# Where the lower half of V's token sums stands: partition 1, written by a transfer, or partition 32, written in place

## The chip, the cores and the metric

The kernel runs on one core of a Trainium2 chip. The time is device microseconds for one execution; lower is better. A core has TensorE (PE in the profile; its weight loads are the row PEld), VectorE (DVE), ScalarE (ACT), GpSimd (POOL) and the queue SP, from which this kernel issues all its transfers. The profile is one execution recorded on the chip.

## The reference, cut to what matters

Two stages follow each other. The first is attention with a bucket mask, for 4 batches and 8 heads of 768 tokens with 64 columns each; the second is a mixture of 4 causal attention experts on the result, per batch, of which each token uses two.

```python
q_bits = (np.einsum('bhsd,dk->bhsk', q, proj) > 0)          # six sign bits: a bucket of 64
mask = q_bucket[:, :, :, None] == k_bucket[:, :, None, :]
scores = scale * np.matmul(q, k.transpose(0, 1, 3, 2))
scores = np.where(mask, scores, -1000000000.0)
scores = scores - np.max(scores, axis=-1, keepdims=True)
attn = np.exp(scores)
attn = attn / (np.sum(attn, axis=-1, keepdims=True) + 1e-09)
return np.matmul(attn, v)
...
logits = x @ w_gate                                          # second stage, per expert e:
scores = np.where(causal, -1000000000.0, scale * (q @ k.transpose(0, 2, 1)))
ye = a @ v @ wo[e]                                           # a: softmax of scores
out += mask[..., None] * w[:, :, kk:kk + 1] * ye
```

One detail matters here. A query whose bucket holds no key has the same score for every key, so its result is the plain mean of V over the 768 tokens. The kernel marks such queries with a flag, and at the end of each head adds flag times (sum of V over the tokens) to the numerator and flag times 768 to the denominator.

## The kernel before, in words

**Units.** The work is cut into 48 units: 32 heads of the first stage (kind "L") and 16 experts of the second (kind "M"). They run in the order of `seq` (line 1393): first the heads of batch 0 by themselves, then the heads of a batch mixed with the experts of the batch before. Two neighbouring heads make a pair, which shares its loads, its scales and its V.

**One unit on TensorE.** The 768 queries and keys are six tiles of 128. `max_steps` (line 959) makes the scores of a unit two units ahead in PSUM tiles `mx`, of which there are two, and VectorE reduces each to row maxima (`pm`, or `pmw` for the first eight heads, which work in fp32). `shift_steps` turns the maxima into rows (`negm`, `row` or `roww`) and, for heads, into flags. `s_unit` (line 1075) makes the scores again with the keys on the partitions, in PSUM tiles `st`, of which there are three; ScalarE takes the exponential twice (`p` in fp32, `ph` in fp16) and GpSimd forms the remainder `pl` = p - ph. Some chunks after that (`LAG` = 4) the products with V follow, into the PSUM tile `o`: `ph` and `pl` with V's upper half `vh`, `ph` with its lower half `vl`. With the last chunk of a head, six more matmuls `o<-vs,fq` add the flagged queries' share (line 1155), and `normalise` divides and frees `o`.

**V's token sums.** `prep_v` (line 907) prepares V once for each pair, 16 times in all. It splits V into halves, sums each over the tokens by matmuls with a column of 2^-10 (`ones`), copies the 128 sums to `vcol`, transposes this column to a row, and writes the row's upper half to partition 0 of `vs` (type fp16). The remainder goes to a row `vsl` on partition 0, and a transfer of 256 bytes carries it to partition 1 of `vs`. The lines are 937 to 944. Two sets of `vs` take turns.

**Flags.** `flags` (line 1014) compares the transposed maxima of 12 rows (two copies of six tiles) and a transfer writes them to partitions 0 and 1 of `fq`, 768 queries wide. All other partitions of `fq` and `vs` are zero from the beginning, so `o<-vs,fq` runs over all 128 partitions and adds upper and lower half in one go.

**The order.** The program does not issue as it is written. A `Recorder` collects every operation with what it reads and writes, and `schedule` (line 310) plays it through on paper: each engine's time for each operation (`_cost`), delays between engines (`LAT`, `WAIT`), the number of buffers, and a priority. On each engine the operations are then issued in the planned order, and every engine works through its own list without overtaking. A transfer also moves one shared clock of the planner on, `dma`, by its size (line 254 and line 395):

```python
run = big.shape[-1] * (2 if big.dtype == HF else 4)
o.dma = prod(big.shape) * (2 if big.dtype == HF else 4) / 360.0 * (2 if run < 512 else 1)
...
dma = end = max(dma, st + 1275.0) + o.dma
```

The planner sees operands as `View`s, and a slice of partitions keeps its first and last one but not its step (line 57):

```python
p0, p1, _ = k[0].indices(self.shape[0])
return self._then("__getitem__", (key,), {}, (self.part[0] + p0, self.part[0] + p1), self.idx[k[1:]])
```

Almost every instruction has line 427 in the profile, since they are all issued there; so tiles, and not lines, tell them apart.

Of the kernel before, what the change touches and what calls it, by code (L numbers as in the profile page):

```python
# [10 lines left out]
FT = mybir.dt.float32  # L11
FR = mybir.dt.float32r
BF = mybir.dt.bfloat16
HF = mybir.dt.float16
I32 = mybir.dt.int32
AF = mybir.ActivationFunctionType
OP = mybir.AluOpType
# [443 lines left out]
def tile_kernel(ctx, tc, q, k, v, proj, w_gate, wq, wk, wv, wo, out):  # L461
    nc = Recorder(tc.nc, loose=("misc",))
    B, HP, _, _, HS = q.shape
    E, Dm, D = wq.shape
    H, S = 2 * HP, 2 * HS
    NB = proj.shape[1]
    NT = S // 128
# [5 lines left out]
    con = Pool(nc, ctx.enter_context(tc.tile_pool(name="con", bufs=1)), 1, 0)  # L473
    sb = Pool(nc, ctx.enter_context(tc.tile_pool(name="sb", bufs=2)), 2, 0)
# [3 lines left out]
    def misc():  # L478
        return psum.tile([128, 512], FT, name="misc", bufs=2)
# [32 lines left out]
    ident = con.tile([128, 128], FT, name="ident")  # L512
# [71 lines left out]
    RW = con.tile([128, 4], FT, name="rw")  # L584
    VS = [con.tile([128, 2, 66], HF, name=f"vs{i}") for i in range(NV)]
    FQ = [con.tile([128, S], HF, name=f"fq{i}") for i in range(3)]
    NM = [con.tile([128, 12, NT], FT, name=f"negm{i}") for i in range(3)]
    tri = con.tile([128, E, E], FT, name="tri")
    rows01 = con.tile([3, 128], HF, name="rows01")
# [12 lines left out]

    def constants():

        for t in NM + FQ:
            nc.gpsimd.memset(t, 0.0)
        for t in PM:
            nc.gpsimd.memset(t, -CLIP)
        nc.gpsimd.memset(NMW, 0.0)
        nc.gpsimd.memset(lower, 1.0 / UNIT)  # L610
        nc.gpsimd.memset(lower[0:NT], 0.0)
        nc.gpsimd.memset(rows01, UNIT)
        nc.gpsimd.memset(rows01[0:1], 0.0)
        for t in VS:
            nc.gpsimd.memset(t, 0.0)
            nc.gpsimd.memset(t[0:1, 0, 0:2], S / 1024.0)
            nc.gpsimd.memset(t[0:1, 1, 64:66], S / 1024.0)
        for t in VH + VF:
            nc.gpsimd.memset(t[:, :, 0:2], 1.0)
            nc.gpsimd.memset(t[:, :, 130:132], 1.0)  # L620
        for t in MVHS:
            nc.gpsimd.memset(t[:, :, :, 64:66], 1.0)
        nc.gpsimd.memset(mask_n, 0.0)
        nc.gpsimd.affine_select(out=mask_n, in_=mask_n, compare_op=OP.is_ge, fill=-BIG, base=0,
                                pattern=[[-1, 128]], channel_multiplier=1)
        nc.gpsimd.memset(mask_t, 0.0)
        nc.gpsimd.affine_select(out=mask_t, in_=mask_t, compare_op=OP.is_ge, fill=-BIG, base=0,
                                pattern=[[1, 128]], channel_multiplier=-1)
        nc.gpsimd.memset(ones, 2.0 ** -10)
        nc.gpsimd.memset(tri, 0.0)  # L630
        for e in range(1, E):
            nc.gpsimd.memset(tri[:, e, 0:e], 1.0)
# [272 lines left out]
    npair = [0]  # L905

    def prep_v(b, hp):
        nat = NAT.pop(("v", b, hp))
        c = CS[b % 2][:, hp, 2:3]
        if not b and hp < 2:  # L910
            mx = sb.tile([128, 1], BF, name="mx")
            nc.gate = marks["row"]
            nc.vector.tensor_reduce(mx, nat.rearrange("p h s -> p (h s)"), axis=AX.X, op=OP.max,
                                    apply_absolute_value=True)
            nc.gate = None
            yield 0
            scale_of([mx], c, 10)
            yield 213
        vs, vh, vl, vf = (t[npair[0] % NV] for t in (VS, VH, VL, VF))
        npair[0] += 1  # L920
        for h in range(2):
            cv = vf[:, :, 2 + D * h:2 + D * h + D]
            nc.scalar.activation(cv, nat[:, h].rearrange("p (j d) -> p j d", j=NT), AF.Copy, scale=c)
            hv = vh[:, :, 2 + D * h:2 + D * h + D]
            nc.scalar.activation(hv, cv, AF.Copy)
            nc.gpsimd.tensor_tensor(vl[:, :, h], cv, hv, op=OP.subtract)
            if not h:
                yield 0
        for h in range(2):
            U["L", b, 2 * hp + h].update(vf=vf[:, :, 66 * h:66 * h + 66], vh=vh[:, :, 66 * h:66 * h + 66], vl=vl[:, :, h], first=2 - 2 * h, den=64 * h,  # L930
                                         order=[2 * (i % 3) + i // 3 for i in range(NT)], c=c, vs=vs[:, h])
        yield 0
        p = misc()
        for n in range(2 * NT):
            x = vl[:, n // 2].rearrange("p h d -> p (h d)") if n % 2 else vh[:, n // 2, 2:2 + 2 * D]
            nc.tensor.matmul(p[:, 0:1], x, ones[:, 0:1], start=not n, stop=n == 2 * NT - 1)
        col = sb.tile([128, 1], FT, name="vcol")
        nc.copy(col, p[:, 0:1])
        nc.tensor.transpose(p[0:1, 128:256], col, ident)
        tv, to = p[0:1, 128:128 + 2 * D], vs.rearrange("p h c -> p (h c)")[:, 2:2 + 2 * D]  # L940
        nc.copy(to[0:1], tv)
        vsl = sb.tile([1, 2 * D], HF, name="vsl", bufs=1)
        nc.vector.tensor_tensor(vsl, tv, to[0:1], op=OP.subtract)
        nc.sync.dma_start(to[1:2], vsl)
        yield 450


# [66 lines left out]
    def flags(d, p):  # L1014
        fr = sb.tile([2 * NT, 128], HF, name="fr")

        if "wide" in d:
            nc.vector.tensor_scalar(fr, p[0:2 * NT, 0:128], WIDE / 2, 1024.0, op0=OP.is_ge, op1=OP.mult)
        else:
            nc.choose(("scalar", "activation", (fr, p[0:2 * NT, 0:128], AF.Relu), dict(scale=2.0 ** -18, bias=-1024.0)),  # L1020
                      ("vector", "tensor_scalar", (fr, p[0:2 * NT, 0:128], CLIP, 1024.0), dict(op0=OP.is_ge, op1=OP.mult)))
        d["fq"] = FQ[nflag[0] % 3]
        nflag[0] += 1
        nc.sync.dma_start(d["fq"][0:2].rearrange("p (j s) -> p j s", j=NT), fr[:, None, :])

    def shift_steps(u):
        d = U[u]
        lsh = u[0] == "L"
        nm = NM[nshift[0] % 3]
        nshift[0] += 1  # L1030
# [38 lines left out]
        if lsh:  # L1069
            flags(d, p)  # L1070
# [343 lines left out]
    for b in range(B):  # L1414
        for hp in range(HP):
            i = pos["L", b, 2 * hp]
# [17 lines left out]
            i = max(pos["L", b, 2 * hp + 1] + 1, i6 + 1 + XTS * hp)  # L1434
# [3 lines left out]
        for e in range(E):  # L1438
            i = pos["M", b, e]
# [5 lines left out]
        i = pos["M", b, E - 1]  # L1445
# [136 lines left out]
```

## Time and profile before

| | |
|---|---|
| median of 3 runs | 619.33 us (618.9 to 621.45) |
| the profiled execution's own time | 619.93 us |
| its span, first to last instruction | 618.2 us |
| TensorE busy | 603.7 us, 98% of the span |
| VectorE, ScalarE, GpSimd busy | 499.4, 501.0, 478.4 us (81%, 81%, 77%) |
| mean clock granted to TensorE | 0.994 of full |
| share of the 16 DMA engines taken by transfers | 30.2% |

The span is shorter than the execution by 1.7 us, which lie outside the first and last instruction. A busy row counts the time in which at least one instruction of the engine was under way; matmuls overlap each other, so one of 193 ns does not occupy TensorE for 193 ns. "idle before, releaser" tells how long an engine stood still ahead of an instruction and what ended that; "granted clock" (PEclk) is the share of full speed at which TensorE was allowed to run.

### The profile page before, as it was taken

How to read it: one execution, taken by the hardware profiler on the slowest of the kernel's cores; microseconds unless marked ns; L12 is line 12 of the kernel's file. 1: busy time of each engine (PE TensorE's matmuls, PEld its weight loads, DVE VectorE, ACT ScalarE, POOL GpSimd, SP SyncE). 2: the span in 40 equal slices, each digit the busy share in tenths (PEclk: the TensorE clock that was granted, in tenths of full speed). 3: DMA queues.
4: the chain of work that ended last, by engine and by line, in shares of the span. 5: the costliest groups of instructions: out<-in, count | busy, mean ns of one | idle time of the engine just before them, and what ended most of it. 6: DMA issues, size and time to landing. Idle time of an engine off the chain costs nothing.

```text
span 618.2 us, 20738 instructions
## 1 busy us (share of the span) xinstructions
PE 603.7 (98%) x7938; PEld 446.0 (72%) x7938; DVE 499.4 (81%) x1217; ACT 501.0 (81%) x1107; POOL 478.4 (77%) x535
## 2 busy tenths in 40 slices
PE   8989999999999999999999999999999999999996
PEld 5678787877777676777676777777776767767673
DVE  5866999999879998988888998996987877446753
ACT  2678799999959898977978989986988978933783
POOL 8788899998948898976976889884995868940560
PEclk9989999999999999999999999999999999999999
DMA  6765722233310414222242413222232221011212
GB/s 188 199 178 135 160 61 96 66 104 97 101 45 23 127 38 128 62 74 49 73 126 68 132 47 106 54 88 65 66 92 83 61 54 29 3 27 47 67 70 103
DMA packets 42931, 52.45 MB, mean 85 GB/s; under 512 B 15081, under 2 KB 32593, under 8 KB 42833
## 3 DMA queue, kind: packets, MB, share of 16 engines
q1 hardware_dynamic: 42833, 51.14, 30.2%
q8 instruction: 62, 1.02, 0.7%
q14 instruction: 36, 0.29, 0.1%
HBM read 20.98 MB, written 6.29 MB: 44 GB/s over the span
## 4 chain that ended last, share of the span: by engine, by line
PE 86%; ACT 5%; DVE 4%; DMA 2%; issue 1%; POOL 1%; SPq 0%; POOLq 0%; ACTq 0%; DVEq 0%
PE misc L427 25%; PE st L427 24%; PE o L427 23%; PE mx L427 14%; ACT p L427 2%; ACT ph L427 2%; DVE pm L427 1%; DMA vs<-vsl 1%; DVE qk L427 1%; POOL pl L427 1%; DMA qk<-Mw 1%; DMA qk<-M 1%; ACT xt L427 0%; DVE yn L427 0%; DVE xt L427 0%
## 5 line engine op out<-in xcount | busy, mean ns | idle before, releaser
L427 POOL TENSOR_TENSOR pl<-p,ph 128x512 f16<-128x512 f32 x368 | 415.7, 1154 | 105.3 <-ACT ph L427 59.3
L427 ACT ACTIVATE p<-st 128x512 f32<-128x512 f32 x372 | 223.9, 602 | 29.9 <-PE st L427 22.6
L427 ACT ACTIVATE ph<-st 128x512 f16<-128x512 f32 x372 | 223.6, 604 | 0.1
L427 DVE TENSOR_REDUCE pm<-mx 128x2 f32<-128x512 f32 (+2 forms) x344 | 203.7, 609 | 19.9 <-PE mx L427 18.9
L427 PE MATMUL st<-qk 128*128 128x256 f16 (+13 forms) x928 | 215.3, 325 | 0.9 <-ACT ph L427 0.6
L427 PEld LDWEIGHTS <-ph 128*128 128x128 f16 x2880 | 151.4, 98 | 26.0 <-issue 4.2
L427 PEld LDWEIGHTS <-qk 78*128 78x128 f16 (+4 forms) x1248 | 111.3, 98 | 49.4 <-issue 4.2
L427 PEld LDWEIGHTS <-pl 128*128 128x128 f16 x1440 | 131.5, 97 | 7.2 <-POOL pl L427 2.7
L427 PE MATMUL mx<-qk 76*128 76x512 f16 (+2 forms) x464 | 129.9, 328 | 1.3 <-DMA qk<-Mw 0.9
L427 PE MATMUL o<-vh,ph 128*128 128x65 f16 (+1 forms) x1104 | 120.1, 194 | 0.5 <-DVE yn L427 0.4
L427 PE MATMUL o<-vh,pl 128*128 128x65 f16 (+1 forms) x1104 | 119.2, 194 | 1.1 <-POOL pl L427 1.0
L427 PE MATMUL o<-vl,ph 128*128 128x64 f16 x1104 | 118.9, 192 | 0.0
L427 PE MATMUL misc<-xt,wqk_h 128*128 128x384 f16 x256 | 54.1, 325 | 0.0
L427 DVE TENSOR_REDUCE pmw<-mx 128x2 f32<-128x512 f32 x68 | 45.3, 681 | 5.8 <-PE mx L427 5.3
L427 PEld LDWEIGHTS <-xt 128*128 128x128 f16 x324 | 30.7, 97 | 10.1 <-DVE pm L427 0.6
L427 PE MATMUL o<-mvh,ph 128*128 128x65 f16 x336 | 36.8, 194 | 0.6 <-DVE yn L427 0.6
L427 PE MATMUL o<-mvh,pl 128*128 128x65 f16 x336 | 36.8, 193 | 0.0
L427 PE MATMUL o<-mvl,ph 128*128 128x64 f16 x336 | 36.7, 192 | 0.0
L427 PEld LDWEIGHTS <-ident 128*128 128x128 bf16 x339 | 28.1, 101 | 10.7 <-issue 2.4
L427 PEld LDWEIGHTS <-wqk_h 128*128 128x128 f16 x256 | 24.3, 97 | 14.6 <-DVE mvl L427 0.2
L427 ACT ACTIVATE qk<-misc 128x384 f16<-128x384 f32 x27 | 13.4, 497 | 23.7 <-PE misc L427 20.2
L427 POOL TENSOR_TENSOR vl<-vf,vh 128x384 f16<-128x384 f32 x32 | 30.4, 954 | 2.6 <-ACT vh L427 2.6
(205 smaller groups left out, 976.9 us busy)
## 6 DMA issues: line engine op xcount, KB each, us to landing
qk<-qk SPq DMA_DIRECT2D x128, 96.0 KB
natv<-in_v_dram SPq DMA_DIRECT2D x16, 384.0 KB
natq<-in_q_dram SPq DMA_DIRECT2D x15, 384.0 KB
natk<-in_k_dram SPq DMA_DIRECT2D x15, 384.0 KB
out_dram<-ot SPq DMA_DIRECT2D x20, 256.0 KB
qk<-qk SPq DMA_DIRECT2D x96, 48.0 KB
xt<-xt SPq DMA_DIRECT2D x16, 96.0 KB
xt<-xt SPq DMA_DIRECT2D x8, 192.0 KB
```

Source lines behind the costliest of these rows:

```text
L427: getattr(getattr(self.nc, e), m)(*[real(x) for x in args], **{k: real(x) for k, x in kw.items()})
```

## The change

The row that the transposition leaves in PSUM becomes 33 partitions high instead of one, with the sums on partitions 0 and 32 and zeros between. For that the column becomes a tile of 33 columns (two constant tiles `vcol0` and `vcol1`, set to zero at the start, which take turns), and the copy writes the sums to its columns 0 and 32. After the transposition one copy writes the 33 rows to `vs`, and VectorE subtracts on partition 32, in place: what stands there in fp16 is replaced by the remainder. The transfer and the row `vsl` are gone. The flags' transfer now writes partitions 0 and 32 of `fq`.

```diff
     FQ = [con.tile([128, S], HF, name=f"fq{i}") for i in range(3)]
+    VC = [con.tile([128, 33], FT, name=f"vcol{i}") for i in range(2)]
...
-        for t in NM + FQ:
+        for t in NM + FQ + VC:
             nc.gpsimd.memset(t, 0.0)
...
-        col = sb.tile([128, 1], FT, name="vcol")
-        nc.copy(col, p[:, 0:1])
-        nc.tensor.transpose(p[0:1, 128:256], col, ident)
-        tv, to = p[0:1, 128:128 + 2 * D], vs.rearrange("p h c -> p (h c)")[:, 2:2 + 2 * D]
-        nc.copy(to[0:1], tv)
-        vsl = sb.tile([1, 2 * D], HF, name="vsl", bufs=1)
-        nc.vector.tensor_tensor(vsl, tv, to[0:1], op=OP.subtract)
-        nc.sync.dma_start(to[1:2], vsl)
+        col = VC[npair[0] % 2]
+        nc.copy(col[:, 0:33:32], p[:, 0:1].to_broadcast([128, 2]))
+        nc.tensor.transpose(p[0:33, 128:256], col, ident)
+        tv, to = p[0:33, 128:128 + 2 * D], vs.rearrange("p h c -> p (h c)")[0:33, 2:2 + 2 * D]
+        nc.copy(to, tv)
+        nc.vector.tensor_tensor(to[32:33], tv[32:33], to[32:33], op=OP.subtract)
         yield 450
...
-        nc.sync.dma_start(d["fq"][0:2].rearrange("p (j s) -> p j s", j=NT), fr[:, None, :])
+        nc.sync.dma_start(d["fq"][0:33:32].rearrange("p (j s) -> p j s", j=NT), fr[:, None, :])
```

## The prediction, as it was put down before the changed kernel ran

> **What bounds the kernel now.** I read the share of busy time first, then what TensorE waited for, then the chain of waits around the one wait that has to do with this change, and last the busy time by stretches there.
>
> ```profile
> span 618.2 us, 20738 instructions
> PE 603.7 (98%) x7938; PEld 446.0 (72%) x7938; DVE 499.4 (81%) x1217; ACT 501.0 (81%) x1107; POOL 478.4 (77%) x535
> ```
>
> TensorE is the bound: it stands still for 618.2 - 603.7 = 14.5 us in all. The waits of TensorE, longest first (us in total, times, longest):
>
> ```profile
> PE o L427 <- DMA vs<-vsl: 2.0, 1, 2.0
> PE o L427 <- DVE ident L427: 1.8, 1, 1.8
> PE st L427 <- ACT ph L427: 1.1, 4, 0.4
> PE o L427 <- POOL pl L427: 1.0, 2, 0.6
> PE o L427 <- DVE yn L427: 1.0, 3, 0.6
> PE mx L427 <- DMA qk<-Mw: 0.9, 1, 0.9
> ...
> PE mx L427 <- DMA qk<-M: 0.2, 1, 0.2
> ```
>
> The longest wait of the run is for the very transfer that the change removes, and it occurs once, though there are 16 such transfers. The timeline shows where:
>
> ```profile
> 35.11 0.27 DVE L427 TENSOR_TENSOR vsl<-misc,vs 1x128 f16<-1x128 f32 x1
> 36.03 0.57 SPq L427 DMA_DIRECT2D vs<-vsl  x1
> 39.11 0.48 PE L427 MATMUL mx<-qk 76*128 76x512 f32 x1
> 41.62 0.34 PE L427 MATMUL o<-vs,fq 128*128 128x66 f16 x6 [2.03 <-DMA vs<-vsl]
> ```
>
> This is the end of the first head. The remainder of V's sums was ready at 35.11 + 0.27 = 35.38 us; the transfer was issued at 36.03, and TensorE's next instruction, the flagged queries' share, could start only at 41.62. In the chain of waits the transfer has one piece, from 36.03 for 5.54 us:
>
> ```profile
> 36.03 5.54 DMA vs<-vsl
> ```
>
> Later pairs have their sums long before a head ends, so nobody waits there. Now the stretches around it (length; busy time and instructions of PE, PEld, DVE, ACT, POOL; granted clock; DMA share; GB/s):
>
> ```profile
> core 0: us, PE busy (x) PEld busy (x) DVE busy (x) ACT busy (x) POOL busy (x), PEclk, DMA share, GB/s
> 24.95:28.37 3.42, 2.54 (x18) 1.93 (x17) 2.42 (x5) 3.42 (x10) 2.52 (x4) 1.00 0.47 127
> 36.00:39.59 3.59, 3.59 (x49) 2.92 (x46) 2.75 (x8) 3.59 (x8) 3.59 (x4) 1.00 0.92 297
> 39.59:41.62 2.03, 0.00 (x1) 0.00 (x1) 0.72 (x2) 2.03 (x5) 2.03 (x4) 1.00 0.53 130
> 41.62:42.02 0.40, 0.40 (x8) 0.40 (x8) 0.02 (x1) 0.06 (x1) 0.40 (x2) 1.00 0.74 181
> 42.02:48.84 6.82, 6.82 (x62) 5.49 (x61) 4.16 (x11) 2.46 (x7) 2.78 (x3) 0.50 0.56 141
> 48.84:52.25 3.41, 3.41 (x39) 3.00 (x36) 2.31 (x4) 3.29 (x8) 3.17 (x3) 1.00 0.53 117
> ```
>
> The stall has a second price. Just after it, from 42.02 to 48.84 us, TensorE's clock is 0.50, and it comes back without any other event. In those 6.82 us ScalarE is busy for 2.46 and GpSimd for 2.78, so TensorE sets the pace, at half speed: 6.82 x 0.5 = 3.41 us of its work is lost. The stretch begins 0.40 us after the stall ended. Mean clock over the span is 0.994 (the table above), a loss of some 0.006 x 618.2 = 3.7 us: there is no second such stretch of that size.
>
> **The change part by part.** *Removed: the transfer, and the wait for it.* The last producer of `vs` becomes VectorE's subtraction, ready at about 35.4 us; TensorE is there at 41.62 - 2.03 = 39.59, with 4.2 us to spare. The stall of 2.03 us goes. Without it nothing in that place holds TensorE still, so I take the half clock to go with it: 3.41 us. Together 5.44 us, the upper end of the gain.
>
> The lower end is what the other engines allow. They have to do the same work in a stretch of 9.25 us (39.59 to 48.84) that would shrink to 9.25 - 5.44 = 3.81. Their idle time in it: VectorE 9.25 - (0.72 + 0.02 + 4.16) = 4.35, ScalarE 9.25 - (2.03 + 0.06 + 2.46) = 4.70, GpSimd 9.25 - (2.03 + 0.40 + 2.78) = 4.04. The rows with the gaps:
>
> ```profile
> 39.62 0.69 DVE L427 TENSOR_REDUCE pmw<-mx 128x2 f32<-128x512 f32 x1
> 42.00 0.22 DVE L427 TENSOR_SCALAR rden<-o,cs 128x6 f32<-128x6 f32 x1 [1.68 <-PE o L427]
> 46.59 0.28 DVE L427 CAST vs<-misc 1x128 f16<-1x128 f32 x1 [1.97 <-PE misc L427]
> 45.38 0.93 POOL L427 TENSOR_TENSOR vl<-vf,vh 128x384 f16<-128x384 f32 x1 [1.51 <-ACT vh L427]
> 49.08 2.28 POOL L427 TENSOR_TENSOR pl<-p,ph 128x512 f16<-128x512 f32 x2 [2.77 <-ACT ph L427]
> ```
>
> So what is late next is VectorE: after the stall it normalises the head (`rden`, `xp`) ahead of the next row maxima, and it can begin this at 39.62 + 0.69 = 40.31 instead of 42.00, only 1.69 us earlier. TensorE has two `mx` tiles, so it feels VectorE soon; GpSimd's remainders are used some chunks later (`LAG`), so its 4.04 us bind less. The gain lies between 4.04 and 5.44 us; I take 4.9, the middle of VectorE's 4.35 and 5.44.
>
> *Removed: 16 issues on SP.* The two kinds of transfers as the tiles' instructions list them (ns least, median, most of the issue):
>
> ```profile
> L427 SPq DMA_DIRECT2D vs<-vsl x16: 552/555/893, 36.0 to 504.1; - x16
> L427 SPq DMA_DIRECT2D fq<-fr x32: 643/698/723, 21.1 to 517.0; - x32
> ```
>
> What stands behind each on SP is issued up to 0.57 us earlier. TensorE's only other wait for a transfer after that point is `qk<-M`, 0.2 us: the gain is 0 to 0.2, taken as 0. The flags' transfer keeps its pieces (12 rows of 256 bytes) and only its target partitions move. The trace shows no transfer to partitions 0 and 32, so I bound its issue by 0.55 us (`vs<-vsl`) and twice its own 0.70, and its landing by the 5.54 us above. No row of TensorE's waits names it, and the first one is issued at 21.1, 18 us ahead of its use: nothing, either way; if that cover were gone, it would cost what `vsl` costs now.
>
> *Changed in size.* Groups by shape (busy us, mean ns, idle before), and one row of a tile's instructions (ns least, median, most):
>
> ```profile
> L427 ACT ACTIVATE vcol<-misc 128x1 f32<-128x1 f32 x11 | 2.4, 220 | 3.9 <-PE misc L427 3.9
> L427 PEld LDWEIGHTS misc<-ident,vcol 128*1 128x1 f32 x16 | 1.4, 85 | 1.3 <-ACT vcol L427 1.0
> L427 PEld LDWEIGHTS misc<-ident,negm x48: 112/114/118, 20.0 to 589.8; 128*72 128x72 f32 x48
> L427 ACT ACTIVATE vs<-misc 1x128 f16<-1x128 f32 x10 | 2.6, 262 | 1.2 <-PE misc L427 1.2
> L427 ACT ACTIVATE fr<-misc 12x128 f16<-12x128 f32 x22 | 5.6, 252 | 0.0
> ```
>
> A column load of 33 lies between those of 1 (85 ns) and 72 (114): at most 0.03 us, 16 times 0.5 us. The copy of 33 rows of 128 instead of one costs the same, as 12 rows take 252 ns against 262 for one; the copy of two columns for one the same 220. The subtraction keeps its shape (0.27 us) and its engine; its result now releases TensorE with no transfer between. The trace shows no subtraction of this shape on partition 32: between 0 and one more instruction's length, 0.27 us, under cover of the 4.2 us to spare in the first pair and of whole heads in the others. I take 0.
>
> [...]
>
> *Added: two memsets on GpSimd at the start.* Bounds: 0.11 us (the 72 columns of `negm`, 0.33 for three) below, 0.2 for both above.
>
> ```profile
> 8.19 0.33 POOL L427 MEMSET negm<- 128x72 f32 x3
> 14.57 1.00 POOL L427 TENSOR_TENSOR qk<-natq,qk 128x384 fp32r<-128x384 f32 x1 [1.18 <-ACT qk L427]
> ```
>
> The first work behind them that others need starts after a wait of 1.18 us for ScalarE: hidden. Without that cover it costs at most 0.2 us.
>
> *The order.* The planner counts 33 partitions for the flags' slice, since it drops the step. With 768 columns of 2 bytes, divided by 360 and doubled for runs of 256 bytes, its price goes from 2 x 768 x 2 / 360 x 2 = 17 ns to 33 x 768 x 2 / 360 x 2 = 282 ns, 32 times, and 16 issues of 570 ns vanish from its SP. So all engines' orders from 21 us on may come out a little different, on paper only. That costs nothing by itself; what a new order can do on the chip is the open term: at best a part of the other waits above (1.1 + 1.0 + 1.0 + 0.9 + 0.2 = 4.2 us, of which I allow a third, 1.3), at worst new stalls like the one at 39.59, 5.44 us each.
>
> The sum against the profiled execution: 619.93 - 4.9 = 615.0. The median is 0.60 below that execution, so 619.33 - 4.9 = 614.4.
>
> **The rivals.**
>
> *The half clock stays, chance 0.09.* The stall goes, but the clock falls for another reason. For it: in 24.95 to 28.37 TensorE stood still for 3.42 - 2.54 = 0.88 us and the clock held, so not every gap does it, and I have a single case. Against it: the fall comes 0.40 us after the longest gap inside the kernel. Time: 619.33 - 2.03 = 617.3. [...]
>
> *One new stall, chance 0.17.* The new order brings another instruction of TensorE too early for its data. For it: the new planner prices above, and thin places such as `qk<-M`, already waited for by 0.2 us. Against it: in 48 units only six rows of TensorE's waits reach 0.9 us in total. Time: 619.33 - 4.9 + 2.03 = 616.5 if the clock holds, 619.33 - 4.9 + 5.44 = 619.9 if not.
>
> *Slower: the new order breaks the cover of the pair's first transfers, chance 0.18.* Place: the signs `qk<-M` that go ahead of a new pair's row maxima. If these slip by 2 us behind other transfers on SP, TensorE stands still as it did at 39.59 and pays the half clock as well, 5.44 us each. One such place gives 619.9, no change; it decides from two, with 619.33 - 4.9 + 10.88 = 625.3. For it: the 0.2 us already there. Against it: there are 16 issues fewer ahead of them on SP.
>
> *The change does not do what it says, chance 0.06.* TensorE stands still at the same instruction, for the flags or a subtraction that the planner put off behind row maxima. Against it: 18 us and 4.2 us to spare. Time: unchanged, 619.3.
>
> **How the numbers follow.** The forecast, 614.4, has 0.50; the four rivals the other 0.50. Its own range is 613.3 to 616.5: below, 619.33 - 5.44 - 0.2 with 0.4 for the runs' lower spread (618.9); above, 619.33 - 4.04 with 1.2 for half of the upper spread. The whole range goes to 612.0 (the 1.3 us of a luckier order) and to 620.5 (one new stall with its half clock, 619.9, and 0.6 of spread); outside lies mainly the slower rival. A measurement of this kernel can tell about 0.5%, 3.1 us, from no change: faster means below 616.2, slower above 622.4. Faster: nearly all of the forecast (0.48) and a few hundredths of the one stall with full clock: 0.52. Slower: 0.18. Within 0.5%: the rest, 0.30.
>
> **What would show each step.** TensorE's waits have no row with `vs`; `o<-vs,fq` of the first head starts right behind a matmul of `mx`, near 39.6 us; the stretches from there to 49 us have clock 1.00 (the 3.41 us are right) or 0.50 (first rival). If the gain is below 4.0 us with full clock, VectorE or GpSimd shows no idle time from 40 to 45. The copy of 33 rows takes 0.25 to 0.28 us, the column's load 0.09 to 0.11. The prediction is wrong if TensorE has a new wait of 1 us or more behind 42 us, or a half-clock stretch elsewhere.

## The result, and the profile after

The changed kernel takes 626.22 us (median of 15 executions, 623.04 to 631.36) against 621.45 us of the kernel before, run beside it (15, 618.54 to 631.82). The ratio is 1.0106, 95% interval [1.0076, 1.0136]: slower by about 1%, where 4.9 us less were forecast. Its profiled execution took 624.08 us. The ratio is not that of these two medians, because executions at a lower clock that take over 1.5% more than their kernel's fastest are left out of it (and out of the medians in the table below, and the profiles of experiments e1 and e7, which are of that kind, are not read).

The share of busy time after the change:

```profile
span 622.3 us, 20709 instructions
PE 602.4 (97%) x7938; PEld 443.4 (71%) x7938; DVE 504.3 (81%) x1212; ACT 503.8 (81%) x1112; POOL 477.0 (77%) x537
```

TensorE stands still for 622.3 - 602.4 = 19.9 us, 5.4 more than before. What it waited for (us in total, times, longest):

```profile
PE mx L427 <- DVE pm L427: 3.6, 8, 0.9
PE mx L427 <- DMA xt<-Mw: 1.9, 1, 1.9
...
PE misc L427 <- DVE negm L427: 1.4, 1, 1.4
...
PE mx L427 <- DMA qk<-M: 0.4, 1, 0.4
```

The row with `vs` is gone. The largest new rows are three: the row maxima wait for VectorE eight times (3.6 us), once for the sign bits of a wide pair (one of those that work in fp32; 1.9), and once `negm` is late (1.4). The stretches tell where. First of the kernel before, then of the one after (length; busy time and instructions of PE, PEld, DVE, ACT, POOL; granted clock; DMA share; GB/s):

```profile
30.00:48.00 18.00, 15.97 (x207) 13.08 (x199) 12.21 (x32) 11.02 (x25) 13.30 (x13) 0.83 0.65 172
48.00:62.00 14.00, 13.94 (x178) 11.68 (x177) 9.05 (x18) 13.75 (x29) 12.72 (x12) 0.97 0.52 132
...
107.00:150.00 43.00, 42.83 (x576) 32.58 (x575) 41.24 (x95) 41.57 (x97) 40.02 (x39) 1.00 0.35 93
```

```profile
30.00:48.00 18.00, 17.88 (x269) 15.42 (x265) 14.35 (x33) 16.86 (x38) 17.04 (x17) 1.00 0.75 198
48.00:62.00 14.00, 10.88 (x123) 7.52 (x123) 8.99 (x17) 9.30 (x19) 11.86 (x12) 1.00 0.71 189
...
107.00:150.00 43.00, 39.76 (x539) 29.28 (x536) 41.90 (x86) 41.10 (x95) 39.27 (x38) 1.00 0.28 74
```

Length less TensorE's busy time is its standstill. From 30 to 48 us it falls from 2.03 to 0.12, and the clock is full: the part that was forecast. From 48 to 62 it rises from 0.06 to 3.12, and from 107 to 150 from 0.17 to 3.24. The sum over the span: standstill +5.4 us; no half clock in the middle of the kernel, -3.4; and TensorE busy for 602.4 us at full clock against 603.7 - 3.41 = 600.3 before, +2.1. Together +4.1, which is 622.3 - 618.2. The 2.1 us are read from matmuls whose ends are modelled; the first after a wait shows its whole length (0.38 us for `mx`) where in a stream the next one starts 0.22 us later, so a part of them belongs to the new waits, and the rest stays open.

### The profile page after: what moved, and what is told of

The parts are those of the page before. It is cut to its first block, busy times and chain, and to the rows that moved or that the text cites. A ratio compares the mean times of both kernels' runs of the same rounds, so it can differ in the third digit from the quotient of the medians.

```text
span 622.3 us, 20709 instructions
## 1 busy us (share of the span) xinstructions
PE 602.4 (97%) x7938; PEld 443.4 (71%) x7938; DVE 504.3 (81%) x1212; ACT 503.8 (81%) x1112; POOL 477.0 (77%) x537
## 3 DMA queue, kind: packets, MB, share of 16 engines
q8 instruction: 62, 1.02, 0.7%
## 4 chain that ended last, share of the span: by engine, by line
PE 72%; DVE 15%; ACT 6%; issue 2%; DMA 2%; POOL 1%; SPq 0%; DVEq 0%; POOLq 0%; ACTq 0%
PE misc L427 23%; PE st L427 19%; PE o L427 18%; PE mx L427 12%; DVE pm L427 5%; DVE qk L427 2%; ACT ph L427 2%; ACT p L427 2%; DVE misc L427 1%; DVE xt L427 1%; POOL pl L427 1%; DVE rden L427 1%; DVE xp L427 1%; DMA qk<-M 1%; DMA wst<-in_moe_wk_dram 1%
## 5 line engine op out<-in xcount | busy, mean ns | idle before, releaser
L427 ACT ACTIVATE qk<-misc 128x384 f16<-128x384 f32 x30 | 15.0, 500 | 24.4 <-PE misc L427 24.2
L427 DVE SCALAR_TENSOR_TENSOR qk<-misc,qk 128x384 f16<-128x384 f32 x32 | 17.7, 552 | 19.0 <-ACT qk L427 19.0
```

The costliest lines, as they stand in the source:

```text
L427: getattr(getattr(self.nc, e), m)(*[real(x) for x in args], **{k: real(x) for k, x in kw.items()})
```

## The experiments

The diff changes two things at once: the instructions that make the sums, and, since the transfer leaves the planner's plan, the order of all engines from then on. (The planner, run on paper, says which part of the change does that. With the flags priced as 2 partitions instead of 33 its order is that of after, but for one instruction of GpSimd and two of TensorE. With the transfer kept beside all the other new instructions it is the order of before.) Most kernels below therefore keep one plan and issue other instructions in its places, by a table that the recorder reads:

```diff
-        for o, (e, m, args, kw, _) in self.schedule():
-            getattr(getattr(self.nc, e), m)(...)
+        for o, (e, m, args, kw, _) in self.schedule():
+            for e, m, args, kw in (self.swap[o](e, m, args, kw) if o in self.swap else [(e, m, args, kw)]):
+                getattr(getattr(self.nc, e), m)(...)
```

All results in one table. Standstill of TensorE is the length of the stretch less its busy time in the profiled execution, in us; the ratio is to the kernel before in the same session. The median of the kernel before differs by up to 3 us between sessions, so kernels are compared within one (e1 to e5, e6 to e8, e9 to e11, e12 to e14, e15 to e17, e18 to e20) or by their ratios.

| kernel | order | median us (n) | ratio [95%] | 30-48 | 48-62 | 62-107 | 107-150 |
|---|---|---|---|---|---|---|---|
| before | old | 620.03 (10) | 1 | 2.03 | 0.06 | 0.94 | 0.17 |
| after | new | 626.22 (15) | 1.0106 [1.0076, 1.0136] | 0.12 | 3.12 | 0.65 | 3.24 |
| e1 in place | old | 623.36 (11) | 1.0008 [0.9967, 1.0049] | | | | |
| e2 transfer | new | 628.91 (5) | 1.0121 [1.0077, 1.0166] | 1.67 | 2.29 | 0.73 | 2.90 |
| e5 after, no wait for weights | new | 629.87 (6) | 1.0162 [1.0111, 1.0214] | 0 | 2.65 | 0.76 | 3.25 |
| e6 after, copies on ScalarE | new | 625.13 (12) | 1.0075 [1.0039, 1.0111] | 0 | 1.53 | 0.77 | 2.01 |
| e7 in place, copies on ScalarE | old | 620.69 (11) | 1.0001 [0.9970, 1.0031] | | | | |
| e8 transfer, copies on ScalarE | old | 622.13 (11) | 1.0030 [0.9996, 1.0064] | 2.25 | 0 | 1.02 | 0.16 |
| e9 = e7, weights later | old | 622.95 (11) | 1.0015 [0.9986, 1.0043] | 0.04 | 0.77 | 1.98 | 0.20 |
| e10 = e8, weights later | old | 623.11 (12) | 1.0010 [0.9980, 1.0040] | 1.61 | 0.76 | 1.57 | 0.17 |
| e11 = e6, weights later | new | 627.14 (12) | 1.0086 [1.0058, 1.0113] | 0 | 0.46 | 3.40 | 2.00 |
| e12 after, short maxima | new | 625.22 (12) | 1.0054 [1.0019, 1.0090] | 0 | 3.07 | 0.74 | 3.24 |
| e13 in place, short maxima | old | 619.44 (11) | 0.9948 [0.9913, 0.9983] | 0 | 1.24 | 0.93 | 0.18 |
| e14 transfer, short maxima | old | 619.78 (12) | 0.9964 [0.9928, 1.0000] | 1.71 | 0 | 0.97 | 0.19 |
| e15 after, GpSimd short | new | 622.41 (12) | 1.0019 [0.9983, 1.0054] | 0 | 3.30 | 0.22 | 2.10 |
| e16 transfer, GpSimd short | old | 618.27 (10) | 0.9957 [0.9925, 0.9990] | 1.36 | 0 | 0.61 | 0.03 |
| e17 in place, GpSimd short | old | 619.34 (12) | 0.9974 [0.9942, 1.0006] | 0 | 2.79 | 0.64 | 0.02 |
| e18 in place, no weight loads | old | 624.53 (11) | 1.0045 [1.0010, 1.0081] | 0 | 0.83 | 4.52 | 0.19 |
| e19 transfer, no weight loads | old | 626.80 (6) | 1.0104 [1.0051, 1.0157] | 2.32 | 0 | 0.94 | 0.18 |
| e20 = e6, short weight maxima | new | 627.44 (6) | 1.0119 [1.0065, 1.0173] | 0 | 1.70 | 0.76 | 1.47 |

### Instructions and order apart (e1, e2)

e1 issues the new instructions in the order of before: the column copy writes columns 0 and 32, the transposition gives 33 rows, the subtraction works on partition 32, and where the transfer stood nothing is issued. e2 is the reverse, the transfer kept in the order of after.

```diff
+        nc.swap[sub] = lambda e, m, x, k: [(e, m, (to33[32:33], tv33[32:33], to33[32:33]), k)]   # e1
+        nc.swap[dma] = lambda *x: []
...
+        nc.swap[sub] = lambda e, m, x, k: [(e, m, (VSLX, tv[0:1], to[0:1]), k),                  # e2
+                                           ("sync", "dma_start", (to[1:2], VSLX), {})]
```

> The in-place sums with the issue order of the kernel before: the planner still plans the transfer, it is only not issued, and everything else stands in the same order on every engine. Theory 1 (the instructions of the change gain what was forecast, the new order loses it): 614 to 617 us where the kernel before takes 619 to 621, a ratio of 0.990 to 0.996; no wait of TensorE for vs, and units after the first head earlier by 2 to 5 us to the end. Theory 2 (the subtraction on partition 32 and the copy of 33 rows cost VectorE time, 16 times): slower than before as the changed kernel is, a ratio of 1.005 to 1.012.

> The transfer of the kernel before, with the issue order of the changed kernel; the transfer is issued right behind its subtraction. Theory 1 (the order costs): as slow as the changed kernel or slower, 624 to 632 us, since the stall for vs may come back on top. Theory 2 (the new instructions cost): close to the kernel before, 618 to 622 us.

In the old order the new instructions come out even with the transfer, 1.0008, which neither theory had; in the new order the kernel is slower with the transfer too, 1.0121. So the order carries the loss, and the sums written in place gain nothing measurable in either; no kernel here that computes everything is faster than before. That leaves two questions: where the gain goes in the old order, and what the new order costs.

### The new order: waits for weights, and copies of q and k (e5, e6, e7, e8)

In after, VectorE waits 2.08 us for a load of weights at 48 us and `negm` stands behind that. e5 lets the four maxima of wq and wk read a constant tile, so that nothing waits there and the scale of these weights is another. e6, e7 and e8 put the scaled copies `qk<-natq` that VectorE had been given on ScalarE (seven in the new order), in the new order, in place in the old, and with the transfer in the old.

```diff
+            nc.swap[o] = lambda n, m, x, k: [(n, m, (x[0], other), k)]                            # e5
...
+            nc.swap[o] = lambda e, m, y, k, cn=cn: [("scalar", "activation", (y[0], y[1], AF.Copy), dict(scale=cn))]
```

> The changed kernel in its own order, but the four row maxima over the experts' weights read a constant of the same shape that has been there since the start, so VectorE never waits for the weights' transfers; the weights' scale is then another one, the work is the same. If those waits (3.5 us on VectorE around 46 to 52 us) are the main loss: 618 to 622 us. If the loss comes from VectorE's list between 75 and 200 us, where it is the bound: within 1.5 us of the changed kernel, 622.5 to 626 us.

> The changed kernel in its own order, but the scaled copies of q and k that the planner gave to VectorE (7 of 48 in pairs prepared from fp32 loads) are issued on ScalarE at the same place. Theory (VectorE's copies and remainders of q and k wait for a gap between GpSimd's instructions, and the new order puts them where there is none): 619 to 623.5 us, 1 to 5 us below the changed kernel's 626. Rival (the order itself, other waits): within 1 us of the changed kernel.

> In-place sums in the order of the kernel before, and the 6 scaled copies of q that VectorE had are issued on ScalarE at the same place. Theory (in e1 the gain of the removed stall was lost at one such copy, which took 5.21 us): 613 to 617 us, a ratio to the kernel before of 0.987 to 0.995, and 2 to 5 us below e8. Rival (ScalarE's 6 x 0.64 us more work, or another limit, takes the gain): 619 us or more.

> Control for e7: the kernel before, transfer and all, with the same 6 copies on ScalarE. In the profiled execution of the kernel before those copies had little to wait for (5.0 us for 6), so: 618 to 621 us, a ratio of 0.995 to 1.003, with the stall for vs still there. If it comes out below 617, the copies cost the kernel before as well.

e5 is no faster than after (1.0162), and its standstill from 48 to 62 us stays at 2.65: the wait for the weights is not the cause of the loss, the signs `xt<-Mw` are late anyway. e6 takes 1.2 us off the standstill from 107 to 150 us and 1.6 off that from 48 to 62, but stays at 1.0075; the new order costs 4.4 us between e6 and e7 (625.13 - 620.69). e8 against e7 again shows no difference beyond the measurement: the gain that e7 was to show did not come.

### Weights' loads moved behind the signs (e9, e10, e11)

The four loads of wq and wk (seven in the new order) that stand on SP ahead of the third wide pair's signs are issued behind them; their maxima read the constant tile, so that the scale of these weights is another.

```diff
+            if self.until and a[0] == "sync" and o.outs and o.outs[0].tile.name == "wst":
+                held.append((o, a))
+                continue
```

> e7 (in-place sums, order of the kernel before, scaled copies on ScalarE) with the four transfers of the experts' weights that stand on SP ahead of the third pair's signs (xt<-Mw) issued behind them; the weights' row maxima read a constant, so that nobody waits for these. Theory (in e1 and e7 the gain of the removed stall is lost at xt<-Mw, which is late because SP is still issuing): TensorE's wait there falls from 2.2 us to below 0.5, 613 to 617 us, 3 us or more below e7's 620.9. Rival (the start is bound by something else in turn, the loads of q and k or VectorE): 619 us or more, with a new wait.

> Control for e9: the kernel before with the same copies on ScalarE and the same four transfers later. Its stall for vs stays and makes TensorE late, so xt<-Mw was in time: within 1 us of e8's 622.3. If it is faster by 2 us or more, the later weights help by themselves.

> e6 (the changed kernel in its own order, scaled copies on ScalarE) with its seven transfers of weights ahead of the third pair's signs issued behind them, and the weights' row maxima from a constant. Theory: the waits for xt<-Mw (1.3 us) and negm go and with them the half clock that they bring in some executions: 618 to 622.5 us, 2.5 us or more below e6's 625.1. Rival (the order of VectorE's list from 75 us on costs whatever happens ahead of it): 624 us or more.

The standstill from 48 to 62 us falls to 0.77 and 0.46, and more of it appears from 62 to 107 us (1.98 and 3.40; the control e10 has 1.57 there, so part of that comes with the edit itself). The two kernels in the old order are equal (622.95, 623.11), and the new order is 4.2 us above. Moving transfers within SP's queue only moved the place of the wait.

### Is VectorE's list too full in the new order? (e12, e13, e14)

The 38 maxima of the loads of q, k and v read 128 of the 768 columns, so that the loads' scales come from a part of the data.

```diff
+            nc.swap[o] = lambda e, me, x, k: [(e, me, (x[0], x[1][:, 0:128]), k)]
```

> The order of after, with the 38 maxima of the loads of q, k and v (0.94 us each on VectorE) reading 128 of the 768 columns, so that the loads' scales come from a part of the data; about 0.7 us less of VectorE for each, some 4.5 us of it between the ends of units 5 and 12. Theory A, VectorE's list sets the pace there in the new order: the lag against the kernel before, which grew by 4.3 to 5.3 us in the four kernels with this order, grows by 2 us or less, TensorE's waits there for the row maxima (2.8 us in after) fall below 1, and the median is 621 to 623. Theory B, the order makes TensorE wait for things that do not come from a full VectorE (a transfer, a dependency put too late): the growth stays at 4 us or more and the median at 625 to 627.

> Control: sums in place in the order of before, with the same short maxima. In that order TensorE is the bound between units 5 and 12 and VectorE has room. Theory A: nothing changes against the same kernel with whole maxima, 1.0008 of before, so 620 to 623, and its lag between units 5 and 12 stays within 1 us. Theory B: the same. If shorter work of VectorE is worth 3 us or more here too, the bound by VectorE is not peculiar to the new order, and theory A's reading of the first kernel falls.

> Second control: the kernel before, transfer and order kept, with the same short maxima. Both theories: 619 to 622, with the stall for V's sums near 40 us unchanged at 1.6 to 2.2 us. If it is faster than the in-place kernel in the same order by 2 us or more, in place sums cost something by themselves.

Theory A falls. VectorE is busy for 2.1 us less between 107 and 150 us (39.77 against 41.90), but TensorE's standstill there is the same 3.24, and its lag behind the kernel before grows by 5.6 us between units 5 and 12, as after's own does by 5.3 (counted from 0; the end of a unit is where VectorE begins to write its result `xp` or `yn`). In the old order the lag does not grow (-4.28 to -4.04 in e13). Compared with its own control the new order costs 625.22 - 619.44 = 5.8 us. So the length of VectorE's list is not what costs; the traces below show what stands ahead of a row maximum in it.

e13 also shows where the gain goes in the old order. At the end of the second head its TensorE is 5.4 us ahead of before; behind the wait for the signs of the third pair it is 4.3 us ahead, and at the end 2.1 us; the largest single loss between these is a wait of 1.0 us for the transfer `qk<-qk` at 557 us.

This is after's timeline of VectorE at the two places (start, length):

```profile
109.50 2.53 DVE L427 TENSOR_SCALAR qk<-natq,cs 128x384 f16<-128x384 f32 x1
111.94 0.68 DVE L427 TENSOR_REDUCE pm<-mx 128x2 f32<-128x512 f32 x1
...
142.89 1.21 DVE L427 TENSOR_REDUCE mw<-wst 128x1 bf16<-128x1024 f32 x1
...
144.21 0.68 DVE L427 TENSOR_REDUCE pm<-mx 128x2 f32<-128x512 f32 x1
```

and in TensorE's:

```profile
112.67 0.38 PE L427 MATMUL mx<-qk 76*128 76x512 f16 x1 [0.88 <-DVE pm L427]
...
144.95 0.39 PE L427 MATMUL mx<-qk 76*128 76x512 f16 x1 [0.56 <-DVE pm L427]
145.68 0.38 PE L427 MATMUL mx<-qk 76*128 76x512 f16 x1 [0.34 <-DVE pm L427]
```

One copy of 2.53 us stands ahead of a row maximum and holds TensorE for 0.88 us; one maximum of weights, 1.21 us, ahead of two others costs 0.56 + 0.34. In before a copy of the same kind stood behind six row maxima that came one after the other from 108.11 on, and took 0.91 us; in after five stand ahead of it, from 105.96 on, and the next one waits behind it. In before:

```profile
112.23 0.69 DVE L427 TENSOR_REDUCE pm<-mx 128x2 f32<-128x512 f32 x1
...
112.91 0.91 DVE L427 TENSOR_SCALAR qk<-natq,cs 128x384 f16<-128x384 f32 x1
```

### GpSimd's remainders made short (e15, e16, e17)

The copy of 128x384 took 2.53 us in after and 0.91 in before. It ends (112.03) 0.2 us after one of GpSimd's does, and GpSimd's follow each other up to there without a gap:

```profile
108.41 2.28 POOL L427 TENSOR_TENSOR pl<-p,ph 128x512 f16<-128x512 f32 x2
110.65 1.15 POOL L427 TENSOR_TENSOR wqk_l<-wst,wqk_h 128x512 f16<-128x512 f32 x1
```

The 384 remainders `pl` are replaced by a memset of the same tile, and so left out of the product.

```diff
+                nc.swap[op] = lambda e, m, x, k: [("gpsimd", "memset", (x[0].bitcast(FT), 0.0), {})]
```

> The order of after, with GpSimd's 384 remainders of the exponentials (1.15 us each) replaced by a memset of the same tile, some 0.3 to 0.5 us each, so that the remainders are left out of the product; GpSimd then has gaps between its instructions everywhere. Theory H, VectorE is held by GpSimd's instructions at worse places in the new order: VectorE's 55 copies and remainders of q and k fall from 55.5 us to 40 or less, and the lag against the kernel before with the same edit grows by at most 1.5 us between the ends of units 5 and 12 instead of 4.3 to 5.6; the ratio of the medians of the two is then 0.995 to 1.003. Theory O, the order of the dependencies makes TensorE wait by itself: the lag grows by 4 us or more all the same and this kernel is 3 to 6 us above its control.

> Control: the kernel before with the same memsets in place of GpSimd's remainders. TensorE is the bound there, and GpSimd was not, so both theories expect 616 to 622, with the stall for V's sums near 40 us still there; VectorE's copies and remainders of q and k fall from 50.4 us to 40 or less if GpSimd holds them.

> Sums in place in the order of before, with the same memsets. Both theories: no growth of the lag between units 5 and 12 (1 us or less). If the gain of the start (2.0 us of waiting, 3.4 of half clock) is kept when nothing is held by GpSimd, this kernel is 2 to 5 us below the control with the transfer; if it is eaten by the next transfers all the same, the two agree within 1.5 us.

The copies and remainders of q and k by groups on VectorE (busy us, mean ns), after and then e15:

```profile
L427 DVE SCALAR_TENSOR_TENSOR qk<-natk,cs,qk 128x384 f16<-128x384 f32 x24 | 25.3, 1057 | 0.0
L427 DVE SCALAR_TENSOR_TENSOR qk<-natq,cs,qk 128x384 f16<-128x384 f32 x24 | 24.8, 1034 | 0.1
L427 DVE TENSOR_SCALAR qk<-natq,cs 128x384 f16<-128x384 f32 x7 | 5.3, 751 | 0.0
```

```profile
L432 DVE SCALAR_TENSOR_TENSOR qk<-natq,cs,qk 128x384 f16<-128x384 f32 x24 | 14.8, 618 | 0.5 <-ACT qk L432 0.4
L432 DVE SCALAR_TENSOR_TENSOR qk<-natk,cs,qk 128x384 f16<-128x384 f32 x24 | 14.3, 601 | 0.0
L432 DVE TENSOR_SCALAR qk<-natq,cs 128x384 f16<-128x384 f32 x7 | 2.9, 410 | 0.0
```

They fall from 55.4 to 32.0 us, the same shapes on the same data: VectorE is held by GpSimd, 0.4 us of every 1.04. The lag, here against e16, grows by 3.4 us (1.78 to 5.15) instead of 5.3, the standstill from 107 to 150 us is 2.10 instead of 3.24, and the new order costs 622.41 - 619.34 = 3.1 us against e17, where it was 5.8 with the maxima short. Both theories hold in part: about 1.1 of the 3.1 us of new standstill there come from VectorE held by GpSimd, and the rest remains when it is not. Whether the whole cost falls with it, from 5.8 to 3.1 us, is not shown: each ratio has an interval of some 2 us either way. e17 against e16 (619.34, 618.27): the stall's gain is eaten without GpSimd's hand in it too.

### SP's queue, and the weights' maxima (e18, e19, e20)

e18 (in place) and e19 (transfer), both in the old order, have a memset on GpSimd in place of each of the eight loads of wq and wk, so these weights are a constant. e20 is e6 with the maxima of wv and wo reading a quarter and a half of their columns, so their scales come from a part of them.

```diff
+                nc.swap[o] = lambda e, m, x, k: [("gpsimd", "memset", (x[0], 0.05), {})]         # e18, e19
...
+        nc.swap[o] = lambda e, me, x, k: [(e, me, (x[0], x[1][:, 0:1]), k)]                      # e20
```

> Sums in place in the order of before, and the eight loads of wq and wk replaced by memsets of the same tiles on GpSimd, so that these weights are a constant; eight issues of some 0.6 us leave SP's queue, four of them between 47 and 52 us. Theory Q, SP's queue makes the signs of the next wide pair late: they are issued some 2 us earlier, TensorE stands still for 0.5 us or less between 48 and 62 us instead of 1.3 to 2.8, and the gain of the stall is kept: 2 to 4 us below the control in the median, about 2 us below it between executions at a clock of 0.998 or more. Theory P, the work that makes the signs is late itself: 1 us or more of standstill stays between 48 and 107 us beyond the control's, and the two kernels agree within 1 us.

> Control: the kernel before, with the same eight memsets in place of the loads of wq and wk. Both theories: the stall for V's sums near 40 us stays at 1.4 to 2.3 us, since its transfer stands ahead of those loads on SP; no standstill of 0.5 us or more between 48 and 62 us; 618 to 622.

> The order of after, with the seven scaled copies of q and k that VectorE had on ScalarE, and the maxima of wv and wo (1.2 us each, at 117 and 141 us) reading a quarter and a half of their columns, so that these weights' scales come from a part of them. Theory L, long instructions of VectorE stand ahead of row maxima: TensorE's standstill between 107 and 150 us, 3.2 us in after and 2.0 us with the copies alone, falls to 1.3 or less, and the median is 0.5 to 1 us below the 1.0075 of the kernel with the copies alone. Otherwise it stays at 1.7 or more.

SP's queue in e13, which keeps the loads, ahead of the signs (start and length of the issue):

```profile
47.98 0.59 SPq L432 DMA_DIRECT2D wst<-in_moe_wk_dram  x1
48.68 1.14 SPq L432 DMA_DIRECT2D xt<-xt  x2
49.92 0.75 SPq L432 DMA_DIRECT2D qk<-roww  x1
50.77 0.59 SPq L432 DMA_DIRECT2D fq<-fr  x1
51.46 1.83 SPq L432 DMA_DIRECT2D xt<-Mw  x2
```

and in e18:

```profile
50.74 1.83 SPq L432 DMA_DIRECT2D xt<-Mw  x2
```

In e13 one issue follows the other with 0.1 us between, and TensorE stands still for 1.25 us ahead of the first `mx<-xt`, at 53.90. (The profile puts this wait down to `issue`; by after's 2.35 us from issue to landing, 51.46 + 2.35 = 53.81 is when the signs landed.) In e18 the signs leave 0.7 us earlier, not 2, and no instruction waits for them. But TensorE also came later to that place, by a wait of 0.83 us for a remainder `pl` of GpSimd, which also has the added memsets to do. So the queue is worth 0.7 of the 1.25 us here: theory Q holds for this place in part. The gain is not kept; the profile of e18 shows what took it, on VectorE, GpSimd and TensorE:

```profile
78.12 5.23 DVE L432 TENSOR_SCALAR qk<-natq,cs 128x384 f16<-128x384 f32 x1
...
83.46 0.68 DVE L432 TENSOR_REDUCE pmw<-mx 128x2 f32<-128x512 f32 x1
```

```profile
75.71 4.55 POOL L432 TENSOR_TENSOR pl<-p,ph 128x512 f16<-128x512 f32 x4
80.20 0.94 POOL L432 TENSOR_TENSOR vl<-vf,vh 128x384 f16<-128x384 f32 x1
81.08 1.17 POOL L432 TENSOR_TENSOR pl<-p,ph 128x512 f16<-128x512 f32 x1
82.19 0.94 POOL L432 TENSOR_TENSOR vl<-vf,vh 128x384 f16<-128x384 f32 x1
```

```profile
PE mx L432 <- DVE pmw L432: 4.0, 1, 4.0
```

The copy came to VectorE while GpSimd had work without a gap and ended only at 83.35 us, 0.22 after the last of it (82.19 + 0.94 = 83.13). TensorE waited 4.0 us for the row maximum behind it. In e13 the same copy, in the same place of the same order, started at 78.39 and took 1.15 us. e18 and e19 differ by 2.3 us in their medians, as theory Q would have it, but their intervals overlap and e19 has six executions only, so this is not shown. Both are slower than before (1.0045 and 1.0104), where 618 to 622 us were expected for e19; why stays open.

e20: the standstill from 107 to 150 us falls to 1.47, not quite to the 1.3 expected; the 0.56 us at 144.95 is gone and the 0.34 behind it stays. The rest are three waits for `ph` (0.8 in all) and one for `vcol` (0.2). Its median (627.44, six executions, one of them at a full clock) went the wrong way and does not bear out the 0.5 to 1 us.

### What an execution's clock does

Each execution of the experiments' sessions has its mean clock on record. Of 150 executions of the kernel before in them, 22 had 0.998 or more; their median is 618.64 us. Of after's 15 it was 6, median 624.17. With short maxima, e13 had 7 of 12 (618.5) and e14 4 of 12 (618.8). Over all kernels with sums in place it was 50 of 148 executions, over all with the transfer 33 of 210. At full clock, then, the old order with sums in place is worth some 0.3 us (e13 against e14) and the change as made costs 624.17 - 618.64 = 5.5. Most executions with the stall have some half clock, but only one execution in five more is freed of it when the stall goes.

## Why the prediction was wrong, point by point

*The stall and its place: right.* `o<-vs,fq` of the first head starts without a wait, right behind the head's own products and not behind a matmul of `mx`, 1.8 us earlier than forecast, and TensorE's waits have no row with `vs`:

```profile
37.80 0.19 PE L427 MATMUL o<-vh,pl 128*128 128x66 f16 x1
37.83 0.34 PE L427 MATMUL o<-vs,fq 128*128 128x66 f16 x6
...
54.92 0.71 PE L427 MATMUL mx<-xt 76*128 76x512 f32 x3 [1.88 <-DMA xt<-Mw]
```

The end of the first head comes 3.79 us earlier (41.96 to 38.17) and that of the second 4.58 (57.07 to 52.49), close to the 4.9 forecast.

*The sizes: nearly right.* The tiles' instructions after the change (ns least, median, most):

```profile
L427 PEld LDWEIGHTS misc<-ident,vcol x16: 107/110/115, 32.4 to 505.8; 128*33 128x33 f32 x16
L427 POOL MEMSET vcol<- x2: 131/132/132, 10.5 to 10.5; 128x33 f32 x2
L427 DVE TENSOR_TENSOR vs<-misc,vs x16: 284/284/285, 33.9 to 506.6; 1x128 f16<-1x128 f32 x16
L427 ACT ACTIVATE vs<-misc x11: 252/273/330, 41.9 to 487.6; 33x128 f16<-33x128 f32 x11
L427 SPq DMA_DIRECT2D fq<-fr x32: 541/586/620, 20.6 to 520.7; - x32
```

The column's load takes 110 ns (0.09 to 0.11 forecast), the copy of 33 rows 273 (0.25 to 0.28), the subtraction on partition 32 284 ns, 0.015 us more than before. The two memsets, 0.132 us each, are a little over the upper bound of 0.2 for both, and hidden. The flags' issue, put between 0.55 and 1.40 us and taken as no change, fell from 698 to 586 ns. (Two slips in the prediction's working change little: a third of 4.2 us is 1.4 and not 1.3, and half of the runs' upper spread is 1.06 and not 1.2.)

The term taken as 0, a price of partition 32 on VectorE, can be seen. The subtraction and the instruction behind it, in before and then in after:

```profile
140.53 0.27 DVE L427 TENSOR_TENSOR vsl<-misc,vs 1x128 f16<-1x128 f32 x1
140.73 0.54 DVE L427 TENSOR_SCALAR qk<-misc 128x384 f16<-128x384 f32 x1
```

```profile
139.74 0.28 DVE L427 TENSOR_TENSOR vs<-misc,vs 1x128 f16<-1x128 f32 x1
140.06 1.29 DVE L427 TENSOR_REDUCE pm<-mx 128x2 f32<-128x512 f32 x2
```

In before the second starts 0.07 us ahead of the subtraction's end, in after some 0.03 us behind it. In after none of the 16 subtractions starts before the instruction ahead of it has ended (13 of 16 do in before), and all 16 instructions behind one start after its end (two of 16 in before). So the subtraction on partition 32 overlaps neither neighbour, and in most pairs stands 0.03 us from each; no run tells why. As an estimate from these rows it costs 0.1 us on either side, 3.2 us of VectorE in 16 pairs at most. That is covered: with the order kept, kernels with the sums in place and with the transfer agree within the measurement (e13 and e14, e17 and e16).

*The step that failed first: that 4.9 us gained at 39.6 us are 4.9 us at the end.* The lower end of the gain was worked out from the idle time of VectorE, ScalarE and GpSimd, and SP's queue was looked at for `qk<-M` alone. What was late next was the signs of the next wide pair. In before they were just in time. SP and TensorE there, and from after's chain of waits the time from the issue of the first of the two to its landing:

```profile
54.88 0.70 SPq L427 DMA_DIRECT2D fq<-fr  x1
55.68 1.82 SPq L427 DMA_DIRECT2D xt<-Mw  x2
```

```profile
58.15 0.71 PE L427 MATMUL mx<-xt 76*128 76x512 f32 x3
```

```profile
52.44 2.35 DMA xt<-Mw
```

By these 2.35 us the first of the two lands in before at 55.68 + 2.35 = 58.03, and the matmul that needs it starts 0.12 us later, at 58.15, without a wait. In after TensorE comes to it 5.1 us earlier (54.92 - 1.88 = 53.04), but the transfer is issued only 3.24 us earlier: what stands ahead of it on SP leaves issue behind issue. So 1.9 us of the gain turn into waiting in after (1.25 us in e13, 2.79 in e17), and among the kernels with sums in place that wait is gone only in e18. This is the rival "one new stall", 2.03 us in its price, but at a place that it did not name and in nearly every kernel with sums in place.

*The half clock: right in the trace, mis-sized as a term.* From 30 to 48 us the clock is 1.00 instead of 0.83. But the 3.41 us were taken as certain, except for the first rival's 0.09. Of the executions with the transfer 16% have a clock of 0.998 or more, without it 34%; the half clock stands elsewhere, at other waits (13.65 us of it from 57.15 in e17, 6.83 from 83.13 in e18, where the clock is 0.92 from 62 to 107 us), and the stall for V's sums in e2, 1.6 us, left it at 1.00 from 30 to 48 us.

*The open term of the new order: wrong, and the largest error.* "That costs nothing by itself" was wrong by 3 to 6 us: 5.8 (e12 against e13), 4.4 (e6, e7), 4.2 (e11, e9), and 3.1 (e15, e17), where the intervals overlap. The slower rival had the sign, a chance of 0.18, and nearly the time (625.3 against 626.2), but neither place nor mechanism, so the time is luck: the signs `qk<-M` are waited for by 0.4 us only. The traces show the new standstill in two places. From 48 to 62 us it is 3.07 in e12 against 1.24 in e13: seven loads of weights stand on SP ahead of the signs instead of four, and `negm` comes behind a maximum that waits for one of them. From 107 to 150 us it is 3.24 against 0.18: the order puts a long instruction of VectorE ahead of row maxima, a copy that, beside GpSimd, takes 2.53 us, and a maximum of weights of 1.21 us. Of the 3.1 us there e6 takes away 1.2 and e15 1.1 (in the main the same waits), and e20, on top of e6, 0.5 more; what is left in e20 are single waits of 0.2 to 0.4 us, most of them for `ph`. That these waits make up the whole of the 3 to 6 us is not shown: no kernel in the new order came out even with its control, and the part of the 2.1 us of longer busy time stays open too.

*The price of 33 partitions,* named as a reason for the new order, moves three instructions of it; the transfer's leaving the plan moves the rest.

## What to carry to other kernels

A gain at a stall reaches the end only if the next thing that the stalled engine needs can come earlier too: look for the next instructions that start just in time, and follow their data back through the queue that issues the transfers, not only through the compute engines. Where a planner writes the order, an edit that takes one operation out is two changes; run the new instructions in the old order and the old ones in the new, before either is credited. And an average of busy time says nothing on a list's order: between 107 and 150 us 2.1 us less work for VectorE left TensorE's standstill as it was, while one long instruction ahead of a row maximum cost 0.9 us.

## What the runs showed of the hardware

*Beside GpSimd, most of VectorE's copies and remainders ended a fixed time behind one of its instructions, and could sit through several of them.* The copy of 128x384 takes 0.41 us with GpSimd out of the way (e15, mean of 7), and 0.91 (before), 1.15 (e13), 2.53 (after) and 5.23 us (e18) beside it. In after 5 of the 6 copies that overlap an instruction of GpSimd end 0.22 to 0.24 us after one of GpSimd's ends, and 40 of the 44 remainders 0.41 to 0.42 us after. The other five take 0.41 and 0.60 to 0.61 us, as the five without any overlap do (0.41, and 0.57 to 0.61). In e18 at least three of GpSimd's instructions began while the copy was under way (80.20, 81.08 and 82.19); they take 0.94 to 1.17 us each, so it sat through several.

*Inside the kernel the half clock lasted 3.41 us or a multiple of it in these runs, and did not follow from the length of a standstill.* 6.83 us (before, 42.02 to 48.84, at 0.50), 10.24 (e19, whose clock is 0.78 from 30 to 48 us and 0.92 from 48 to 62) and 13.65 us (e17, whose PEclk is 0.8 and 0.7 in the two slices from 46.7 to 77.8) are seen: 2, 3 and 4 times 3.41. Gaps of 2.03 (before), 2.32 (e19) and 2.79 us (e17) had it behind them; behind gaps of 1.25 (e13), of 2.1 and 1.6 (e2, up to 48 us), of 1.36 and 1.88 us 5 us apart (after), and of 2.1 us (e12) the clock of the stretch was 1.00, yet one of 1.36 us (e16) had 3.41, with a clock of 0.91 from 30 to 48 us.

*The issue of a transfer of 3 KB to partitions 0 and 32 took 586 ns where that to partitions 0 and 1 took 698* (after and before, medians of 32). In the old order it was 0.58 and 0.59 us in place (e13, both rows from 42 to 51 us) and 0.69 and 0.71 with the transfer (e19, from 43 to 55); no run tells why.
